# Attention with a relative position bias and a squared-ReLU layer: longer score matmuls, block diagonals, and x transposed by DMA

## Chip, core and metric

The kernel runs on one core of one Trainium2 chip. The time is the device time of one execution in microseconds (us). Before the change the median of three runs was 442.41 us (440.94 to 442.55). The engines are named as in the profile: PE (TensorE), PEld (its weight loads), ACT (ScalarE), DVE (VectorE), POOL (GpSimd), SP (SyncE). POOL and SP issue the DMAs.

## What is computed

Eight batches, eight heads, 576 positions, head size 64: attention with a bias that depends on the distance of query and key alone, then two dense layers on the 4608 tokens of 512 values, with a squared ReLU between them.

```python
scores = scale * np.matmul(q, k.transpose(0, 1, 3, 2))          # 8 x 8 x 576 x 576
scores = scores + bias.transpose(2, 0, 1)[None, :, :, :]        # bias_table[bucket(|i - j|)]
attn = np.exp(scores - max); attn = attn / attn.sum(-1)
x = np.matmul(attn, v)                                          # -> (4608, 512)
h = np.maximum(x @ w_in, 0.0)                                   # w_in 512 x 2048
return h * h @ w_out                                            # w_out 2048 x 512
```

Beyond a distance of 128 all pairs share one bucket, so the kernel multiplies the exponentials by a table only in a band around the diagonal, and leaves the common factor to the normalization. Inputs are float32, cast to fp16 by the load DMAs.

## The kernel before

**Work in pairs of heads.** A pair p is a batch b and two heads (`pair`, 32 of them). The q and k of a batch are staged by load DMAs from POOL (`stg`, two buffers). For each pair PE transposes five blocks of q and five of k against an identity (L504) into a PSUM bank `f`; ACT or DVE copies them out to `qt` and `kt` (L483, L485), with one head on partitions 0 to 63 and the other on 64 to 127. Scores come transposed, keys on partitions: for each of four key blocks and each half of the queries (288) two matmuls, one per head, each on its 64 rows of PE (L528), into one of two score buffers `st` of two banks each. The last 64 keys make a set of their own of four matmuls (L535). ACT takes the exponential of each set, 576 columns at a time, nine per pair (L554), into `pt` and `pm`. DVE multiplies the bands by the table (L574). PE then forms PV for five blocks of queries, in a first part of three and a second of two, into the single bank `pv` (L612, L619); a column of ones in v gives the sum of each row. DVE takes the reciprocal (L636) and writes normalized x (L641).

**The dense layers.** After the four pairs of a batch, `x_turn` transposes x in 20 blocks on PE (L663) and ACT or DVE copies it to `xt`, a ring of 2560 tokens. A group g is 512 tokens, nine in all: f1 is 16 times four matmuls of 512 columns (L758), ACT takes the ReLU (L778), DVE squares it into `g` (L786); f2 is 16 quarters of four matmuls (L707); ACT or DVE copies `y` out (L727, L733) and SP stores it (L741). Transposes, f1 and f2 share three banks `f`.

**The order.** Nothing is issued as it is written. Each step is an operation in a plan (`Plan`) with the engines that may do it, an estimated cost, its dependencies, its buffers and a due time; `schedule` repeatedly takes the operation that can start first, the due time deciding ties, and the program is emitted in the planned order. Each engine works through its own instructions in that order. A pair's due time grows by `FAST` for the first pairs and by `PERIOD` after that, and `after` forbids work too far ahead of it. On PE an operation has a mode: "r" and "q" are the score matmuls on half the rows, "f" is full-array work; the plan adds `SWITCH` where the mode changes.

**The start.** On SP the small bias table is loaded, one matmul spreads it over distances, DVE casts it (L289), SP writes it to DRAM (`t_bias`) and reads it back skewed (`tr_sb`, four DMAs, all at L243), and DVE copies it into the tables (L314, L323). POOL issues the loads: `load_pair` for batch 0, `load_qk`, `load_v`, and the weights. Loads wait for DVE's memsets, the weight loads for nothing.

Of the kernel before, what the change touches and what calls it, by code (L numbers as in the profile page):

```python
# [27 lines left out]
XR = 2560  # L28
# [43 lines left out]
LAT = {"PE": 200.0, "ACT": 90.0, "DVE": 90.0, "POOL": 120.0, "DMA": 0.0, "SP": 0.0}  # L72
SWITCH = 60.0


class Plan:
# [11 lines left out]
    def schedule(self):  # L88
        engines = ("PE", "ACT", "DVE", "POOL", "SP", "DMA")
# [57 lines left out]
    @staticmethod  # L147
    def _buf_time(op):
        t = 0.0
        for b in op.bufs:  # L150
            if b.slot is None:
                if not b.ring.free:
                    return float("inf")
                t = max(t, min(b.ring.free)[0])
        return t


def mm(n):
    return n / 2.4 + 2.5
# [11 lines left out]
def kernel(  # L171
# [37 lines left out]
    tr_sb = sb("tr_sb", [128, H, 384])  # L209
    tv_sb = sb("tv_sb", [H, 512])  # L210
    oh_sb = sb("oh_sb", [32, 512])
    NSTG, NQK, NPT, NV, NX, NGB, NRT, NY = 2, 5, 2, 3, 2, 2, 4, 3
    stg = [[sb(f"{n}s{i}", [128, 5, 512]) for n in "qk"] for i in range(NSTG)]
    qts = [sb(f"qt{i}", [128, S]) for i in range(NQK)]
    kts = [sb(f"kt{i}", [128, S]) for i in range(NQK)]
# [5 lines left out]
    xs = [sb(f"x{i}", [128, 5, 512]) for i in range(NX)]  # L221
    xt_sb = sb("xt", [128, 4, XR])
    gs = [sb(f"g{i}", [128, 16, GT]) for i in range(NGB)]
    rts = [sb(f"rt{i}", [128, GT]) for i in range(NRT)]
# [14 lines left out]
    def loader(eng_name, eng, out_, in_, packets, deps=(), bufs=(), due=0.0):  # L239
# [8 lines left out]
        return P.add({"DMA": packets * 27.0 / 16}, None, [issue], bufs, due), issue  # L248
# [4 lines left out]
    def load(eng_name, eng, out_, in_, packets, deps=(), bufs=(), due=0.0):  # L253
# [12 lines left out]
    l_bt = load("SP", nc.sync, const(bt_sb), const(bias_table), 32, due=0)  # L266
    l_far = load(
        "SP", nc.sync, const(far_sb), const(bias_table[NBK - 1 : NBK, :].to_broadcast([NBK, H])), 32, due=1
    )
    l_oh = load("SP", nc.sync, const(oh_sb), const(oh_d.ap()), 32, due=2)  # L270
    l_id = load("SP", nc.sync, const(id_sb), const(id_d.ap()), 128, due=3)
# [21 lines left out]
    o = load("SP", nc.sync, lambda: tdram.ap(), const(tv_sb), 64, [o])  # L293
    o = P.add({"SP": 2000.0}, None, [o])
# [6 lines left out]
            256,  # L301
# [31 lines left out]
    first = []  # L333
    for i in range(NSTG):
        for w in range(2):
            first.append(
                P.add({"DVE": 320.0}, lambda i=i, w=w: io(nc.vector.memset(stg[i][w][64:128, 4, :].bitcast(FP32), 0.0)), due=10 + i)
            )
    for i in range(NPT):
        first.append(P.add({"DVE": 90.0}, lambda i=i: io(nc.vector.memset(pts[i][:, PW:], 1.0)), due=20))  # L340
        first.append(P.add({"DVE": 90.0}, lambda i=i: io(nc.vector.memset(p4s[i][:, S:], 1.0)), due=20))
# [30 lines left out]
    def load_pair(b, w, hp):  # L372
        src = (q, k)[w]
        t = lambda: stg[b_stg[b].slot][w]
        ls = []
        for h in (2 * hp, 2 * hp + 1):
            ls.append(
                load(
                    "POOL", nc.gpsimd,
                    lambda h=h: t()[:, 0:4, ts(h, D)],  # L380
                    const(src[b, h, 0:512, :].rearrange("(t p) d -> p t d", p=128)),
                    512, first[0:4], [b_stg[b]], pdue(),
                )
            )
        ls.append(
            load(
                "POOL", nc.gpsimd,
                lambda: t()[0:64, 4, ds(128 * hp, 128)].rearrange("p (h d) -> p h d", d=D),
                const(src[b, 2 * hp : 2 * hp + 2, 512:576, :].transpose([1, 0, 2])),
                128, first[0:4], [b_stg[b]], pdue(),  # L390
            )
        )
        l_qk[b, w, hp] = ls
# [451 lines left out]
```

## Time and profile before

| | |
|---|---|
| median of 3 runs | 442.41 us (440.94 to 442.55) |
| the profiled execution | 443.17 us |
| its span, first to last instruction | 441.4 us |
| busy PE / ACT / DVE / POOL | 417.2 / 288.0 / 210.2 / 119.5 us |
| chain that ended last, by engine | PE 91%, DMA 3%, ACT 3%, DVE 2%, issue 1% |
| granted TensorE clock, mean | 0.996 |
| DMA | 29.24 MB in 122170 packets |

The profile is of one execution. "Busy" adds the durations of an engine's instructions; matmuls are pipelined, so a busy PE says only that one was under way. The chain is followed back from the last instruction, at each step to what released it. In a group's row, the text before the bar is line, engine, operation, output<-inputs, shapes and count; behind it stand the busy time and mean duration (ns), then the engine's idle time just before these instructions and who ended it. In the rows of stretches each engine has its busy time and its instruction count.

### The profile page before, as it was taken

Reading aid. Unit: us, or ns where it says so; the run is one execution under the profiler, and the core shown is the slowest. Engines: PE = TensorE matmul, PEld = TensorE weight load, DVE = VectorE, ACT = ScalarE, POOL = GpSimd, SP = SyncE. Lnnn points to the kernel's source line nnn. Section 1 sums busy time; section 2 is a strip of 40 time slices with the busy share of each in tenths; the row PEclk is TensorE's granted clock in tenths of the full one; section 3 lists DMA queues with packets and bytes.
Section 4 is the critical chain, followed back from the end, with each engine's and each line's share of the span. In section 5 each row is a group of like instructions: output and inputs, shape, how many; then the busy total and the mean of one; then the engine's idle time right before and its main releaser. Section 6 shows DMA issues by size and latency. Waiting matters only on the chain.

```text
span 441.4 us, 9092 instructions
## 1 busy us (share of the span) xinstructions
PE 417.2 (95%) x3713; PEld 209.7 (48%) x3713; DVE 210.2 (48%) x513; ACT 288.0 (65%) x495; POOL 119.5 (27%) x154
## 2 busy tenths in 40 slices
PE   1687999999999999999999999999999999999996
PEld 0265545554455445544454445544454454544442
DVE  3545556445555655455455446465544553352210
ACT  1657787667866876777767666685777766464421
POOL 7998569422162205230254007000000000000000
PEclk9998999999999999999999999999999999999999
DMA  9999999918091808980099009400010001000111
GB/s 131 159 87 165 190 166 122 137 29 76 2 133 28 74 1 74 108 55 24 26 133 79 1 25 113 68 1 25 25 50 1 25 24 49 25 25 25 48 49 72
DMA packets 122170, 29.24 MB, mean 66 GB/s; under 512 B 113896, under 2 KB 117008, under 8 KB 122128
## 3 DMA queue, kind: packets, MB, share of 16 engines
q0 software_dynamic: 115552, 18.36, 56.5%
q1 hardware_dynamic: 6576, 10.30, 6.7%
q8 instruction: 29, 0.48, 0.5%
q14 instruction: 13, 0.11, 0.1%
HBM read 37.55 MB, written 9.45 MB: 106 GB/s over the span
## 4 chain that ended last, share of the span: by engine, by line
PE 91%; DMA 3%; ACT 3%; DVE 2%; issue 1%; SPq 0%; ACTq 0%; DVEq 0%
PE f L707 30%; PE f L758 29%; PE st L528 11%; PE pv L619 9%; PE f L504 4%; PE pv L612 3%; PE st L535 3%; PE f L663 2%; ACT pt L554 2%; DMA tr_sb<-t_bias 1%; DMA t_bias<-tv_sb 1%; DMA oh_sb<-c_oh 1%; SPq L243 0%; DVE pt L574 0%; ACT y L727 0%
## 5 line engine op out<-in xcount | busy, mean ns | idle before, releaser
L554 ACT ACTIVATE pt<-st 128x576 f16<-128x576 f32 x256 | 157.3, 649 | 42.1 <-PE st L528 40.1
L707 PE MATMUL f<-w_out_sb,g 128*128 128x512 f16 x576 | 144.9, 380 | 0.4 <-ACT qt L483 0.3
L758 PE MATMUL f<-xt,w_in_sb 128*128 128x512 f16 x576 | 141.0, 380 | 0.9 <-DVE xt L485 0.4
L778 ACT ACTIVATE rt<-f 128x512 f16<-128x512 f32 x144 | 86.1, 598 | 57.1 <-PE f L758 53.2
L786 DVE TENSOR_TENSOR g<-rt 128x512 f16<-128x512 f16 x144 | 61.1, 425 | 100.6 <-ACT rt L778 100.4
L758 PEld LDWEIGHTS <-w_in_sb 128*128 128x128 f16 x576 | 51.0, 97 | 61.3 <-issue 3.8
L574 DVE TENSOR_TENSOR pt<-pt,tb_sb 128x512 f16<-128x512 f16 (+2 forms) x96 | 59.7, 623 | 40.7 <-ACT pt L554 37.7
L707 PEld LDWEIGHTS <-g 128*128 128x128 f16 x576 | 48.7, 98 | 60.8 <-issue 13.2
L528 PE MATMUL st<-qt,kt 64*128 64x288 f16 x512 | 66.2, 298 | 4.8 <-ACT pt L554 3.7
L243 POOL DMA_DIRECT2D qs<-in_q_dram x47 | 38.1, 834 | 101.4 <-PE f L504 98.1
L619 PE MATMUL pv<-va,pt 128*128 128x65 f16 x1280 | 57.2, 196 | 0.2 <-DVE pt L574 0.2
L619 PEld LDWEIGHTS <-pt 128*128 128x128 f16 x1280 | 52.6, 100 | 5.1 <-issue 0.7
L528 PEld LDWEIGHTS <-kt 64*128 64x128 f16 x512 | 20.2, 94 | 57.8 <-issue 52.9
L243 POOL DMA_DIRECT2D va<-in_v_dram x32 | 28.4, 916 | 43.0 <-PE pv L619 26.9
L243 POOL DMA_DIRECT2D ks<-in_k_dram x47 | 38.2, 858 | 6.3 <-DMA w_out_sb<-in_moe_w_out_dram 3.5
L612 PE MATMUL pv<-vm,pm 128*128 128x130 f16 x160 | 36.1, 225 | 0.2 <-DVE x L641 0.2
L641 DVE TENSOR_TENSOR x<-pv,r 128x384 f16<-128x384 f32 x64 | 31.4, 491 | 2.2
L554 ACT ACTIVATE pm<-st 128x576 f16<-128x576 f32 x32 | 20.8, 651 | 13.0 <-PE st L535 13.0
L636 DVE RECIPROCAL r<-pv 128x6 f32<-128x6 f32 x64 | 11.9, 187 | 26.0 <-PE pv L619 25.7
L727 ACT ACTIVATE y<-f 128x512 f32<-128x512 f32 x20 | 12.0, 598 | 18.6 <-PE f L707 18.2
L504 PE MATMUL f<-id_sb,qs 128*128 128x128 f16 x160 | 15.5, 234 | 4.3 <-DMA qs<-in_q_dram 4.3
L612 PEld LDWEIGHTS <-pm 128*128 128x128 f16 x160 | 15.9, 99 | 6.5 <-issue 1.4
(37 smaller groups left out, 175.7 us busy)
## 6 DMA issues: line engine op xcount, KB each, us to landing
out_dram<-y SPq DMA_DIRECT2D x36, 256.0 KB, 2.0
va<-in_v_dram POOLq DMA_DIRECT2D x32, 128.0 KB, 5.2
qs<-in_q_dram POOLq DMA_DIRECT2D x28, 128.0 KB, 4.6
ks<-in_k_dram POOLq DMA_DIRECT2D x28, 128.0 KB, 5.1
w_in_sb<-in_moe_w_in_dram POOLq DMA_DIRECT2D x4, 512.0 KB, 7.4
w_out_sb<-in_moe_w_out_dram POOLq DMA_DIRECT2D x4, 512.0 KB, 9.5
qs<-in_q_dram POOLq DMA_DIRECT2D x15, 64.0 KB, 4.8
ks<-in_k_dram POOLq DMA_DIRECT2D x15, 64.0 KB, 4.7
```

Of the source, the lines that this page charges most:

```text
L243: lambda: io(eng.dma_start(out=out_(), in_=in_())),
L504: io(nc.tensor.transpose(ps[:, ts(t, 128)], stg[b_stg[b].slot][w][:, t, ts(hp, 128)], id_sb))
L528: nc.tensor.matmul(ps[:, e, 0:HQ], kt[rows, ts(jt, 128)], qt[rows, ts(hh, HQ)], start=True, stop=True,)
L554: nc.scalar.activation(out=dst, in_=sets_ps[st.slot][:, :, 0:HQ], func=EXPF, scale=SCALE)
L574: io(nc.vector.tensor_tensor(out=a, in0=a, in1=t, op=MULT))
L612: nc.tensor.matmul(ps[:, i, :, :], pm[:, c : c + 128], vm[:, hp, :, 0:65], start=True, stop=False)
L619: nc.tensor.matmul(ps[:, i, e, :], pt[:, (2 * jt + e) * S + c : (2 * jt + e) * S + c + 128], va[:, jt, 2 * hp + e, 0:65], start=False, sto ...
L641: nc.vector.tensor_tensor(out=xs[xb.slot][:, qt0 : qt0 + nq, ts(hp, 128)].rearrange("p t (e d) -> p t e d", e=2), in0=ps[:, :, :, 0:64], i ...
L707: nc.tensor.matmul(g_ps[bank.slot], gs[gb.slot][:, nt, ts(m, 128)], w_out_sb[:, nt, :], start=(nt == 0), stop=(nt == 15),)
L758: nc.tensor.matmul(g_ps[bank.slot], w_in_sb[:, kk, ts(nt, 128)], xt_sb[:, kk, c : c + GT], start=(kk == 0), stop=(kk == 3),)
L778: nc.scalar.activation(out=rts[rb.slot], in_=g_ps[bank.slot], func=RELUF)
L786: nc.vector.tensor_tensor(out=gs[gb1.slot][:, nt, :], in0=rts[rb.slot], in1=rts[rb.slot], op=MULT)
```

## The change

**Scores.** The nine sets of a pair become six. A key block's set now has all of the first 512 queries: two matmuls of 512 columns, one per head on its 64 rows (L604 in the new file). Outside batch 0 the blocks are run two at a time, so that one visit fills both score buffers (`run([0, 1])`, `run([2, 3])`). The last 64 queries go against all four key blocks by four full-array matmuls of 128 columns (L628) with `qz`, in which the 64 last queries of each head stand on a block diagonal; the last 64 keys likewise by two matmuls of 288 columns with `kz` (L653). The off-diagonal blocks of `qz` and `kz` are zeroed once (four buffers each); per pair four copies of 64x64 fill the diagonals (L586), each on DVE or POOL as the plan finds. Exponentials are of 1024 columns (four per pair, L615), 512 (L638) and 576 (L663).

**x.** With `DT_X`, x is laid out per pair and each part of PV is followed by one DMA transpose from SBUF to SBUF, issued by SP (L779): 32 of three blocks and 32 of two. `x_turn` isn't called. `DT_QK = 8` leaves q and k on PE in all eight batches. `xt` is a ring of 2304 tokens; f1 of the one group that crosses its end (group 4) is cut into two times 256 columns.

**Loads.** In batches 0 and 1 q and k are loaded six positions to a partition (96 partitions, 1536 bytes of the source in a row), transposed by 12 matmuls of 96 columns on half the output partitions (L559), and put in order by the evacuating copy. In batches 2 to 7 a batch's q is ten DMAs (one per head, and two for the last 64 positions) in place of five, k the same. The first q and k no longer wait for memsets. POOL's order of loads is new, as the diff shows. The first reading of the table lies in the buffer of `g`, which group 1 overwrites after the table is copied.

**The plan.** New due times, `SWITCH` 105, latencies for DMAs and a new resource "XB" for the transposes; f2 and f1 wait for their own quarter of the weights and squares instead of all.

The diff, cut:

```diff
-XR = 2560
+XR = 4 * S
+DT_QK = 8
+PERIOD, LEAD, FAST, FASTN = 9700.0, 8100.0, 4800.0, 5
+AHEAD, G0, GP = 12500.0, 22300.0, 37900.0
+DT_X = True
...
-LAT = {"PE": 200.0, "ACT": 90.0, "DVE": 90.0, "POOL": 120.0, "DMA": 0.0, "SP": 0.0}
-SWITCH = 60.0
+LAT = {"PE": 200.0, "ACT": 90.0, "DVE": 90.0, "POOL": 120.0, "DMA": 1800.0, "SP": 0.0, "XB": 2000.0}
+SWITCH = 105.0
...
     for hp in range(4):
         for w in range(2):
-            load_pair(0, w, hp)
+            load_six(0, w, 2 * hp, 2)
         if hp == 1:
-            load_v(0)
+            load_v_tail(0, range(4))
+            for h in range(4):
+                load_v_head(0, h)
+    for h in range(4, 8):
+        load_v_head(0, h)
+    for u in range(4):
+        load_w_in(u)
     for w in range(2):
-        load_qk(1, w)
-    for kk in range(4):
-        load_w_in(kk)
+        load_six(1, w, 0, 4)
     load_v(1)
+    for w in range(2):
+        load_six(1, w, 4, 4)
     for u in range(4):
         load_w_out(u)
...
-    PERIOD, LEAD, FAST = 10300.0, 12000.0, 5900.0
...
+        spread = []
+        for w, src, dst in ((0, qts, qzs), (1, kts, kzs)):
+            for e in range(2):
+                rw = ds(64 * e, 64)
+
+                def sp(o, src=src, dst=dst, rw=rw):
+                    eng = nc.vector if o.eng == "DVE" else nc.gpsimd
+                    io(eng.tensor_copy(out=dst[qb.slot][rw, rw], in_=src[qb.slot][rw, 512:576]))
+
+                spread.append(one_of({"DVE": 130.0, "POOL": 300.0}, sp, [evac[w]] + z_fix, [qb], T - 1000))
...
+        def run(jts):
+            sets = [Buf(r_set) for _ in jts]
+
+            def score():
+                kt, qt = kts[qb.slot], qts[qb.slot]
+                for jt, st in zip(jts, sets):
+                    for e in range(2):
+                        rw = ds(64 * e, 64)
+                        io(
+                            nc.tensor.matmul(
+                                sets_ps[st.slot][:, e, :], kt[rw, ts(jt, 128)], qt[rw, 0:512],
+                                start=True, stop=True,
+                            )
+                        )
...
+        def last_queries():
+            st = Buf(r_set)
+
+            def score():
+                for jt in range(4):
+                    io(
+                        nc.tensor.matmul(
+                            sets_ps[st.slot][:, 0, ts(jt, 128)], kts[qb.slot][:, ts(jt, 128)], qzs[qb.slot],
+                            start=True, stop=True,
+                        )
+                    )
...
+        if b < 1:
+            run([0])
+            run([1])
+            last_keys()
+            run([2])
+            run([3])
+        else:
+            run([0, 1])
+            last_keys()
+            run([2, 3])
+        last_queries()
...
+            if DT_X:
+                c = (b % 4) * S + 128 * qt0
+                t = P.add(
+                    {"SP": 1000.0},
+                    lambda qt0=qt0, nq=nq, c=c: io(
+                        nc.sync.dma_start_transpose(
+                            out=xt_sb[:, hp, c : c + 128 * nq].rearrange("p (t d) -> p t d", d=128), in_=xs[xb.slot][:, hp, qt0 : qt0 + nq, :].rearrange("p t d -> p (t d)")
+                        )
+                    ),
+                    [o, x_last.get((hp, 1 - part))] + xt_free(b * S + 128 * (qt0 + nq)), [xb], T - 2000,
+                )
+                t = x_last[hp, part] = P.add({"XB": 160.0 * nq}, None, [t], [xb], T - 2000)
...
-        x_turn(b, norms)
+        if not DT_X:
+            x_turn(b, norms)
```

Where instructions come to stand, as the two programs are emitted. First PE in the middle of the program, before: a score visit between two f2 quarters (`g` and `w_out_sb`); `st` is a score buffer, `kt` the turned keys.

```order
L707 MATMUL f_114<-w_out_sb,g_100 128x512
L528 LDWEIGHTS kt_85
L528 MATMUL st_111<-qt_80,kt_85 128x288
L528 LDWEIGHTS kt_85
L528 MATMUL st_111<-qt_80,kt_85 128x288
L707 LDWEIGHTS g_100
```

After, in the same part of the work:

```order
L741 MATMUL pv_117<-va_96,pt_91 128x65
L604 LDWEIGHTS kt_82
L604 MATMUL st_115<-qt_78,kt_82 128x512
L604 LDWEIGHTS kt_82
L604 MATMUL st_115<-qt_78,kt_82 128x512
L604 LDWEIGHTS kt_82
L604 MATMUL st_116<-qt_78,kt_82 128x512
L604 LDWEIGHTS kt_82
L604 MATMUL st_116<-qt_78,kt_82 128x512
L844 LDWEIGHTS g_105
```

A visit holds four matmuls of 512 columns in place of two of 288, and follows PV or f2 as before.

Second, PE where f1 of group 3 begins, before; what an instruction waits for stands in brackets:

```order
L707 LDWEIGHTS g_99
L707 MATMUL f_115<-w_out_sb,g_99 128x512
L758 LDWEIGHTS w_in_sb
L758 MATMUL f_114<-xt,w_in_sb 128x512 [waits DVE_49]
L758 LDWEIGHTS w_in_sb
L758 MATMUL f_114<-xt,w_in_sb 128x512
```

After:

```order
L844 MATMUL f_118<-w_out_sb,g_104 128x512
L897 LDWEIGHTS w_in_sb [waits DMAHW1_49]
L897 MATMUL f_119<-xt,w_in_sb 128x512 [waits DVE_49]
L897 LDWEIGHTS w_in_sb
L897 MATMUL f_119<-xt,w_in_sb 128x512 [waits DMAHW3_49]
L897 LDWEIGHTS w_in_sb [waits DMAHW5_49]
L897 MATMUL f_119<-xt,w_in_sb 128x512 [waits DMAHW4_49]
L897 LDWEIGHTS w_in_sb [waits DMAHW7_49]
L897 MATMUL f_119<-xt,w_in_sb 128x512 [waits DMAHW1_49]
```

The waits on the copies of `xt` (DVE) are replaced by waits on DMA completions (DMAHW); the one on DVE that is left is for the bank.

Third, SP ahead of and among the output stores, before:

```order
L243 DMA t_bias<-tv_sb 8x512 [waits DVE_49]
L243 DMA tr_sb<-t_bias 128x2x384 [waits DMAHW4_49]
L243 DMA tr_sb<-t_bias 128x2x384 x2
L243 DMA tr_sb<-t_bias 128x2x384 [waits DMAHW0_49]
L741 DMA out_dram<-y_105 128x512 [waits DMAHW1_49,Activation_49]
L741 DMA out_dram<-y_106 128x512 [waits DMAHW2_49,DVE_49]
L741 DMA out_dram<-y_107 128x512 [waits DMAHW3_49,DVE_49]
```

After, with the transposes of batch 4:

```order
L779 DMA_TRANSPOSE xt<-x_101 128x3x128 [waits DMAHW4_49,DVE_49,PE_49]
L779 DMA_TRANSPOSE xt<-x_101 128x2x128 [waits DMAHW5_49,DVE_49,PE_49]
L878 DMA out_dram<-y_112 128x512 [waits DMAHW6_49,Activation_49]
L779 DMA_TRANSPOSE xt<-x_101 128x3x128 [waits DMAHW7_49,DVE_49]
L779 DMA_TRANSPOSE xt<-x_101 128x2x128 [waits DMAHW0_49,DVE_49,PE_49]
L779 DMA_TRANSPOSE xt<-x_101 128x3x128 [waits DMAHW1_49,DVE_49]
L878 DMA out_dram<-y_110 128x512 [waits DMAHW2_49,DVE_49]
```

The 64 transposes now stand among the 36 stores in one queue; a transpose waits for DVE's norm, for PE's last use of that part of the ring, and for the DMA eight places ahead, and a store that waits for `y` holds the transposes behind it.

On POOL, 45 of the 128 copies into `qz` and `kz` stand between the loads; the other 83 are on DVE. In batches 2 and later the copies stand right behind loads in five places, in four of them behind 20 or more.

364 lines of the change are left out of this document (209 added, 155 removed).

## Prediction

> **What bounds the kernel now.** I read the page's engine totals first, then its chain of work that ended last, then busy time by stage. The PE row and the chain by engine:
>
> ```profile
> PE 417.2 (95%) x3713; PEld 209.7 (48%) x3713; DVE 210.2 (48%) x513; ACT 288.0 (65%) x495; POOL 119.5 (27%) x154
> PE 91%; DMA 3%; ACT 3%; DVE 2%; issue 1%; SPq 0%; ACTq 0%; DVEq 0%
> ```
>
> PE carries 91% of a 441.4 us chain, about 402 us. Busy time in two stretches (length, then PE, PEld, DVE, ACT, POOL, granted clock, DMA share, GB/s) shows where the rest lies:
>
> ```profile
> 0.00:50.20 50.20, 31.34 (x357) 19.97 (x357) 25.15 (x77) 28.10 (x48) 42.01 (x60) 0.97 1.47 140
> 50.20:420.00 369.80, 368.29 (x3276) 181.95 (x3277) 183.78 (x434) 255.64 (x441) 77.45 (x95) 1.00 0.55 56
> ```
>
> From 50.2 us on PE is full (368.3 of 369.8 us), so the time there is the sum of PE's instructions, with ACT at 69% and DVE at 50%. The chain near 240 us (start, length, what; xN is matmuls) prices each kind:
>
> ```profile
> 234.40 0.23 PE st L528 x2
> 234.63 0.97 PE f L707 x4
> 235.60 0.22 PE f L663 x4
> 235.82 2.59 PE f L758 x12
> 238.41 0.35 PE st L528 x4
> 238.77 1.83 PE f L758 x8
> ...
> 241.80 0.29 PE f L504 x5
> ...
> 244.25 0.06 PE pv L612
> 244.31 0.24 PE pv L619 x8
> 244.55 0.86 PE f L758 x4
> 245.41 0.36 PE st L535 x4
> ```
>
> Twelve 512-column matmuls behind another full-array matmul take 2.59 us, 0.216 each. Four take 0.86 us behind PV, but 0.97 us behind scores: entering full-array work from scores costs 0.107 us more. Two 288-column score matmuls, on the two row halves, take 0.23 us, four take 0.35 us: a second pair adds 0.12 us (one 288-column stream, so the halves run together), and entering the scores costs the other 0.11 us. A change of kind, either way, is 0.107 us. A transpose is 0.056 us (0.22 over four, 0.29 over five), a 65-column PV matmul 0.03, a 130-column one 0.06.
>
> Now the instruction order, which has no times. Before has 383 such changes. Its columns at these prices sum to 364.2 us and 383 x 0.107 = 41.0, together 405.2 us, within 1% of the chain's 402. The same sum up to the first f1 matmul is 19.8 us; that matmul starts at 50.24 us, so 30.4 us are lost ahead of it. What is left of 441.4 is about 4 us at the end and 2 us between.
>
> **The change, part by part.** The profiled execution took 443.17 us, 1.77 more than its span; the median of the runs is 442.41, 0.76 less. I sum against 443.17 and take 0.76 off at the end.
>
> *Fewer changes of kind.* A pair now has two visits to row-tiled scores, mostly four 512-column matmuls at a time; the remaining queries and keys are full-array matmuls on block diagonals and need no change. The order has 144 changes (14 of them around the 96-column transposes of batches 0 and 1, priced alike). 239 x 0.107 = **-25.6 us**.
>
> *Score columns.* Tiled pairs: 256 x 0.1225 = 31.4 us become 128 x 0.216 = 27.6: -3.7. The last keys stay at 0.245 us per pair of heads (two 288-column streams). The last queries are new: 128 x 0.056 = +7.2. **+3.5 us**.
>
> *Transposes.* The 160 of x leave PE: 160 x 0.056 = **-9.0 us**. Those of q and k become 240 at 0.056 and 192 column-tiled ones of 96 columns, 28 ns each if their halves run together: 18.8 against 17.9, with the split f1 group **+1.1 us**.
>
> PE in all: -25.6 + 3.5 - 9.0 + 1.1 = **-30.0 us**, 375 us of work. It counts fully, since PE is full.
>
> *Other engines.* Mean durations of groups (busy us, mean ns):
>
> ```profile
> L554 ACT ACTIVATE pt<-st 128x576 f16<-128x576 f32 x256 | 157.3, 649 | 42.1 <-PE st L528 40.1
> L778 ACT ACTIVATE rt<-f 128x512 f16<-128x512 f32 x144 | 86.1, 598 | 57.1 <-PE f L758 53.2
> L641 DVE TENSOR_TENSOR x<-pv,r 128x384 f16<-128x384 f32 x32 | 17.8, 557 | 1.1
> L636 DVE RECIPROCAL r<-pv 128x6 f32<-128x6 f32 x32 | 6.2, 194 | 16.7 <-PE pv L619 16.6
> L354 DVE MEMSET vm<- 64x8 f16 x6 | 0.4, 65 | 0.3
> L323 DVE COPY tm_sb<-tr_sb 64x192 f16<-64x192 f16 x8 | 2.3, 288 | 0.1
> ```
>
> 64 more columns cost 51 ns, so a 1024-column exponential is about 1.01 us and a pair's six take 4 x 1.01 + 0.60 + 0.65 = 5.28 us against 9 x 0.649 = 5.84. ACT and DVE also lose the 40 evacuations of x. Neither is on the path after 50 us; this counts only at the start. The 128 new 64x64 copies lie between 65 and 288 ns each; 83 stand on DVE, 45 on POOL.
>
> *The start.* Chain pieces and two timeline rows:
>
> ```profile
> 6.80 4.76 DMA t_bias<-tv_sb
> 12.53 5.50 DMA tr_sb<-t_bias
> 25.79 0.22 PE pv L612
> 50.24 2.76 PE f L758 x12
> ```
>
> ```profile
> 1.24 1.25 POOL L243 DMA_DIRECT2D w_in_sb<-in_moe_w_in_dram  x2 [0.79 <-POOLq L829]
> 10.40 0.69 PE L504 MATMUL f<-id_sb,qs 128*128 128x128 f16 x5 [4.34 <-DMA qs<-in_q_dram]
> ```
>
> Before, two 512 KB weight loads stand ahead of the first q, and PE begins at 10.4 us. Now q and k stand first: I take 6.5 us. The table's road is the same two DMAs in series, so the first PV needs about 19 us instead of 25.8, and pair 1 is through at 24.5. Two pt buffers let pair 2's exponentials start only then: 2 x 5.28 = 10.6 brings 35, band and PV of the last pair 3.5, x to f1 4.1: 42.6 us. PE's own work ahead of it is 17.2 us, so 25.4 are lost against 30.4: **-5 us**, from -9 (PE begins at 5, lighter queues) to +2 (the table still decides, and x comes late).
>
> *The wait for x.* Only this kernel's other DMAs from SP bound it (duration of an issue, then of landing; both answers are for the output stores), with the identity's landing under the first loads as the far end:
>
> ```profile
> L741 SPq DMA_DIRECT2D out_dram<-y x36: 332/332/356, 79.9 to 438.3; - x36
> DMA to landing us min/median/max: 2.0/2.0/4.8
> ```
>
> ```profile
> id_sb<-c_id SPq DMA_DIRECT2D x1, 32.0 KB, 7.6
> q0 software_dynamic: 115552, 18.36, 56.5%
> ```
>
> From the end of PV: reciprocal 0.19, norm 0.56, issue 0.33 (one plain issue) to 1.0 (three, one a block), landing 2.0 to 4.8: 3.1 to 6.6 us. In the order, the work that PE still has between the last PV that a group needs and the group's first f1 is 6.9, 5.1, 6.2, 6.2, 5.1, 5.1, 4.9 and 16.4 us for groups 1 to 8 (before group 3: two score runs with their entry and exit 1.3, four quarters of f2 3.5, ten transposes 0.6, a PV part 0.6, the last keys 0.25). Group 0 has none; its wait is in the start. A light queue hides it all; a loaded one leaves 1 to 2 us at up to seven groups. The load queue holds 56.5% of the DMA time, so I take half of the groups at 1 us: **+3 us** (0 to +14). The stores on SP are no hindrance: 36 x 0.33 and 64 issues of at most 1 us are 76 us of 410.
>
> The page "VectorE: DVE Perf Modes" of the Trainium skill (section "The three transpose paths") speaks against this edit: 1309 ns for a 128x128 block through the DMA crossbar, 390 ns on TensorE. The second is not what this stream pays (0.056 us). By the first, an estimate is 3.9 us for three blocks, inside my landing range, and the term would be about the same +3.
>
> *Copies behind loads on POOL.* The q and k of a batch are now 20 loads instead of 10, and some copies that scores need stand right behind them, in a queue whose head waits for PE. From the waits, and the landing of such loads:
>
> ```profile
> POOL qs L243 <- PE f L504: 98.1, 4, 28.7
> va<-in_v_dram POOLq DMA_DIRECT2D x32, 128.0 KB, 5.2
> ```
>
> Each load waits for the one eight places ahead. 20 loads are 4608 packets each for q and k; at 34.5 ns (56.5% of 16 x 441.4 us over 115552 packets) on 16 engines they need 19.9 us, so the end of a burst can be some us later than 20 issues of 0.8. The order has five such places, four of them behind 20 loads or more. Above: 5 x 3; below: 0, if the copies are early. **+4 us**.
>
> *Longer runs need both score buffers at once*, so PE can wait for two exponentials (2 us) where it waited for one. f1 and f2 quarters stand between; the 3.7 us that L528 waited on ACT in all before is the nearest row: **+1** (0 to +6).
>
> ```profile
> L528 PE MATMUL st<-qt,kt 64*128 64x288 f16 x512 | 66.2, 298 | 4.8 <-ACT pt L554 3.7 <-ACT pm L554 0.4
> ```
>
> The end (last output evacuated and stored) is unchanged: 0.
>
> Sum: 443.17 - 30.0 - 5 + 3 + 4 + 1 = 416.2; less 0.76 is 415.4, rounded **415 us**.
>
> The page "TensorE: Matmul & The Clock Gate" of the Trainium skill (Part 1) says that an idle window of about 3.4 us halves PE's clock until it has been busy as long. By that rule the 4.1 us wait ahead of the first f1 would add an estimated 1.7 us. The trace agrees in so far as the clock fell to 0.84 at the start, where PE was busy for 8.44 of 11 us:
>
> ```profile
> 33.00:44.00 11.00, 8.44 (x110) 5.83 (x107) 6.29 (x16) 8.23 (x16) 9.43 (x13) 0.84 1.62 165
> ```
>
> **The rivals.**
> *Late transposes (slower).* Place: the first f1 of each group. If a transpose lands not after 3 us but after T, each of seven groups waits T + 1.25 (reciprocal, norm, issue) less 5.5 us (the mean work in between), and group 0 waits T - 3 more. The other terms save 30 us; slower by 0.5% needs 7 x (T - 4.25) + (T - 3) = 32, that is T = 8.1 us. The identity's 7.6 us comes near it; the stores' maximum of 4.8 us speaks against. At T = 10 it is 460 us.
> *Long row-tiled pairs do not overlap.* Then 128 x 0.216 = 27.6 us come back: 443 us. The 0.12 us of a 288-column pair speaks against.
> *POOL and ACT are late at every batch.* 5 us at each of five burst ends and 6 us for the buffers: 415 + 21 + 5 = 441 at the worst, some 433 in the middle. POOL's 28.7 us wait shows how long its queue can stand.
> *The start doesn't shorten:* 420 us, inside the range.
>
> **How the numbers follow.** The forecast's own range: 443.2 - 30 - 9 = 404, less 0.8 is 403, if nothing new waits; 443.2 - 30 + 2 + 14 = 429 if x is late in all groups. Chances: forecast 0.75, POOL and ACT late 0.12, pairs not overlapped 0.04, late transposes slower than before 0.07, better than 403 0.02. The range 402 to 431 holds the forecast and the nearer part of the third rival. Faster by over 0.5% (2.2 us, about what a measurement of this kernel can tell from no change): 0.75 + 0.12 + 0.02 = 0.89; the pairs' rival is the 0.04 within; slower 0.07.
>
> **What would show it.** Right: PE busy near 390 us or less, the first f1 at 40 to 45 us, four score matmuls of 512 columns at 0.43 us plus one entry in the chain, f1 waiting on the DMA of xt for under 14 us in all, PE full between. Wrong: the DMA of xt ahead of f1 with over 20 us in the waits (T too small), the last keys and queries waiting on POOL for over 10 us, or a four-matmul visit near 0.9 us.

## The result, and the profile after

The changed kernel takes 418.75 us (median, 418.23 to 419.54), the kernel before on the same chip 441.77 us. The ratio is 0.948, with a 95% interval from 0.945 to 0.951. The forecast was 415.0 us, from 402 to 431. The profiled execution took 418.23 us, its span is 416.5 us, 24.9 less than before.

First the engine totals and the chain of the changed kernel, to be laid beside those of before:

```profile
PE 386.6 (93%) x3537; PEld 210.6 (51%) x3537; DVE 213.1 (51%) x576; ACT 271.9 (65%) x387; POOL 157.8 (38%) x241
PE 80%; DMA 9%; POOL 7%; issue 2%; ACT 1%; POOLq 0%; ACTq 0%
```

PE is busy for 30.6 us less. But where DMA, ACT and DVE had 8% of the chain, DMA and POOL now have 16%. These pieces lie ahead of 75.3 us, where the chain runs through POOL's loads and their landings, then through the copies behind them (the two longest landings, and POOL's longest row of issues):

```profile
20.92 17.22 DMA va<-in_v_dram
40.81 13.97 DMA w_out_sb<-in_moe_w_out_dram
57.87 6.58 POOL ks L250 x9
```

Busy time by stage shows the same stretch (length, then PE, PEld, DVE, ACT, POOL, granted clock, DMA share, GB/s), in the changed kernel:

```profile
37.00:82.00 45.00, 31.49 (x310) 16.14 (x307) 20.07 (x52) 25.48 (x38) 34.30 (x51) 0.85 1.62 139
82.00:412.50 330.50, 329.94 (x2900) 178.67 (x2899) 167.17 (x432) 222.11 (x319) 100.00 (x155) 1.00 0.56 66
```

and in the kernel before, with the same borders:

```profile
37.00:82.00 45.00, 42.23 (x430) 23.07 (x428) 25.33 (x60) 34.47 (x61) 34.14 (x43) 0.96 1.84 161
82.00:437.80 355.80, 354.70 (x3096) 175.12 (x3094) 167.87 (x396) 234.64 (x405) 52.66 (x64) 1.00 0.41 48
```

From 82 us on PE is full in both, and all of the gain lies there: 330.5 us instead of 355.8. From 37 to 82 us PE was busy for 42.2 us and is now for 31.5, at a lower clock. PE's waits of 0.2 us and over in that stage, from PE's timeline of the changed kernel (start, length, what, and in brackets the idle time before it and who ended it):

```profile
40.79 0.61 PE L897 MATMUL f<-xt,w_in_sb 128*128 128x512 f16 x1 [3.20 <-DMA xt<-x]
45.70 6.12 PE L897 MATMUL f<-xt,w_in_sb 128*128 128x512 f16 x21 [4.31 <-DMA xt<-x]
64.78 0.88 PE L604 MATMUL st<-qt,kt 64*128 64x512 f16 x4 [0.78 <-ACT pm L663]
67.20 0.39 PE L604 MATMUL st<-qt,kt 64*128 64x512 f16 x2 [0.33 <-ACT pt L615]
69.73 0.22 PE L734 MATMUL pv<-vm,pm 128*128 128x130 f16 x1 [0.61 <-DVE x L763]
75.33 0.42 PE L653 MATMUL st<-qt,kz 128*128 128x288 f16 x2 [3.33 <-POOL kz L586]
```

The first f1 starts at 37.0 us (50.24 before). Two pieces of x come late, 7.5 us in all, and the last keys of a pair wait 3.3 us for a POOL copy. The waits for x are not on the chain above: by it, an earlier x alone would only have PE wait longer for the copy, unless POOL's loads end earlier too. PE's largest waits over the whole run show that both happen in the start and never again (us in total, times, longest):

```profile
PE f L897 <- DMA xt<-x: 7.5, 2, 4.3
PE f L289 <- DMA oh_sb<-c_oh: 4.3, 1, 4.3
PE st L653 <- POOL kz L586: 3.3, 1, 3.3
PE st L604 <- ACT pm L663: 2.0, 4, 0.8
PE pv L741 <- DVE pt L696: 1.9, 3, 0.7
PE st L604 <- ACT pt L615: 1.8, 5, 0.5
```

A simple account follows from the first f1 of group 1, which is the point where PE becomes full. It starts at 100.08 us, before at 100.03 us. In the instruction order PE's work ahead of that point is 61.9 us at the prediction's prices, before 68.75; behind it 313.2 us, before 336.4. So:

| | before | after | difference |
|---|---|---|---|
| PE's work ahead of group 1's first f1 | 68.75 | 61.9 | -6.85 |
| lost ahead of group 0's first f1 (50.24 - 19.8; 37.0 - 17.2) | 30.4 | 19.8 | -10.6 |
| lost between these two | 0.9 | 18.4 | +17.5 |
| from group 1's first f1 to the end of the span | 341.4 | 316.4 | -25.0 |
| span | 441.4 | 416.5 | -24.9 |

The first three rows cancel. Of the 18.4 us, PE's waits of 0.2 us and over make 13.4 (7.5 for x, 3.3 for POOL's copy); an estimated 3.3 us more are a low granted clock behind these two waits, as worked out further down. In the stretch where PE is full, the prices give -23.2 us and the trace -25.0.

Three pieces of the chain of the changed kernel, from that stretch, show the score runs themselves:

```profile
100.94 0.54 PE st L604 x4
103.31 0.24 PE st L653 x2
105.28 0.22 PE st L628 x4
```

Four 512-column score matmuls take 0.54 us: 0.43 for two streams of 512 columns and 0.107 for entering, so the row halves run together. The block diagonals have no entry to pay: 0.24 us for two matmuls of 288 columns, 0.22 for four of 128.

### The profile page after: what moved, and what is told of

Same layout as the page of the kernel before. It is cut to its first block, busy times and chain, and to the rows that moved or that the text cites. A ratio compares the mean times of both kernels' runs of the same rounds, so it can differ in the third digit from the quotient of the medians.

```text
span 416.5 us, 8915 instructions
## 1 busy us (share of the span) xinstructions
PE 386.6 (93%) x3537; PEld 210.6 (51%) x3537; DVE 213.1 (51%) x576; ACT 271.9 (65%) x387; POOL 157.8 (38%) x241
## 4 chain that ended last, share of the span: by engine, by line
PE 80%; DMA 9%; POOL 7%; issue 2%; ACT 1%; POOLq 0%; ACTq 0%
PE f L844 30%; PE f L897 27%; PE pv L741 8%; PE st L604 7%; DMA va<-in_v_dram 4%; PE f L566 4%; DMA w_out_sb<-in_moe_w_out_dram 3%; POOL ks L250 2%; POOL va L250 2%; PE pv L734 2%; DMA ks<-in_k_dram 2%; PE st L653 2%; PE st L628 1%; POOL qs L250 1%; POOL vm L250 1%
## 5 line engine op out<-in xcount | busy, mean ns | idle before, releaser
L615 ACT ACTIVATE pt<-st 128x1024 f16<-128x1024 f32 x128 | 125.3, 1022 | 37.7 <-PE st L604 37.6
L897 PE MATMUL f<-xt,w_in_sb 128*128 128x512 f16 (+1 forms) x640 | 139.1, 361 | 7.7 <-DMA xt<-x 7.5
L897 PEld LDWEIGHTS <-w_in_sb 128*128 128x128 f16 x640 | 60.6, 98 | 67.5 <-issue 8.7
L250 POOL DMA_DIRECT2D qs<-in_q_dram x66 | 47.1, 750 | 47.8 <-PE f L566 36.6
L250 POOL DMA_DIRECT2D ks<-in_k_dram x66 | 47.4, 821 | 0.8 <-DMA ks<-in_k_dram 0.8
L604 PE MATMUL st<-qt,kt 64*128 64x512 f16 x256 | 42.9, 402 | 4.7 <-ACT pm L663 2.0
L864 ACT ACTIVATE y<-f 128x512 f32<-128x512 f32 x30 | 17.9, 598 | 25.6 <-PE f L844 25.3
L586 POOL COPY qz<-qt 64x64 f16<-64x64 f16 x23 | 10.2, 444 | 63.4 <-DVE qt L524 58.6
L663 ACT ACTIVATE pm<-st 128x576 f16<-128x576 f32 x32 | 20.8, 651 | 8.0 <-PE st L653 6.7
L586 POOL COPY kz<-kt 64x64 f16<-64x64 f16 x22 | 7.0, 319 | 39.6 <-DVE kt L524 27.5
L604 PEld LDWEIGHTS <-kt 64*128 64x128 f16 x256 | 8.7, 95 | 23.9 <-issue 20.6
```

The lines of the kernel that those rows point to most:

```text
L250: lambda: io(eng.dma_start(out=out_(), in_=in_())),
L604: nc.tensor.matmul(sets_ps[st.slot][:, e, :], kt[rw, ts(jt, 128)], qt[rw, 0:512], start=True, stop=True,)
L615: nc.scalar.activation(out=p5(pts[pb.slot])[:, jt, :, 0:512], in_=sets_ps[st.slot], func=EXPF, scale=SCALE)
L663: nc.scalar.activation(out=p4s[pb.slot][:, 0:S].rearrange("p (h s) -> p h s", h=2), in_=sets_ps[st.slot][:, :, 0:HQ], func=EXPF, scale=SCALE,)
L897: nc.tensor.matmul(g_ps[bank.slot][:, a:z], w_in_sb[:, kk, ts(nt, 128)], xt_sb[:, kk, c : c + z - a], start=(kk == 0), stop=(kk == 3),)
```

## Experiments

Theory after the result: the gain is the scores' (fewer changes of kind on a full PE), and what was gained on the way to the first f1 is given back right behind it, because x lands late beside the loads and POOL's copies stand behind loads. Rivals: the gain comes from taking x off PE; the losses in the start are ACT's and no queue's; the transposes are slow wherever they stand. "The changed kernel" is the kernel of the diff above; its rows keep its line numbers, and the versions that hold back loads have three lines more ahead of these. PE's work is counted in each order at the prediction's prices. Every ratio is to the kernel before on the same chip, with its 95% interval.

**The changed kernel once more.** 

> The changed kernel as it is, as the yardstick for the three kernels beside it on the same chip: 418.7 us by every theory (418.2 to 419.5 before). The first f1 stalls twice on the DMA of xt (about 3.2 and 4.3 us), the pair at 71 us on the copy into kz (3.3 us).

Measured: 418.48 us, ratio 0.946 (0.944 to 0.948). Here too x was waited for twice (7.4 us) and POOL's copy once (2.5 us).

**The scores as before, the rest as changed.** The scoring loop of the kernel before (nine sets a pair, eight of two matmuls of 288 columns and the last keys' of four, no `qz` and `kz`) in place of the new one:

```diff
-        run([0, 1])
-        last_keys()
-        run([2, 3])
-        last_queries()
+        for jt in (4, 0, 1, 2, 3):
+            for half in range(2) if jt < 4 else (0,):
...
```

> The scores as before the change (288 columns, nine sets a pair, last keys on 64 rows, no block diagonals and no copies into them), everything else of the change kept, the DMA transposes of x too. The order has 369 changes of kind and 395.8 us of PE work against 144 and 375.1. Theory (the scores are most of the gain): +20.7, less the 3 us that PE waited for the copies: 436 to 440 us. Rival (the gain came from x and from the loads at the start): under 430 us.

Measured: 442.49 us, ratio 1.001 (1.000 to 1.003), over both. The new scores are worth 24 us, all of the gain. The 369 changes that I expected leave out those between the last keys' matmuls and the other score matmuls, which are among the prediction's 383. They cost an entry too: in the chain of this kernel the two matmuls of L592 at 133.59 us, right behind the last keys' four, take 0.23 us, which is one pair of 288 columns, 0.12, and 0.11 for entering. With the 23 of these there are 392 changes and 398.3 us of work, so 23.2 of the 24 us are PE's work in the order. The losses differ by only 1 us: the span exceeds PE's work by 42.4 us here and by 41.4 in the changed kernel. The wait for POOL's copy is gone, but PE waits 6.0 us at L592 for exponentials, where the changed kernel waits 3.8 at L604. DMA transposes, loads and plan together bring nothing.

**x on TensorE.** The constant that decides it:

```diff
-DT_X = True
+DT_X = False
```

> The changed kernel with x turned on TensorE again (160 transposes on PE, 40 copies on ACT and DVE; no DMA transposes). The order has 144 changes of kind as before this edit, and 384.1 us of PE work against 375.1. Theory (PE is full after 82 us, so work there counts fully; ahead of that the DMA transposes cost about 7.5 us of waiting, of which a turn on PE gives back some 5): 418.5 + 9 - 5 = 422 to 424 us. Rival 1 (the wait for x would be filled by the loads of batch 1 anyway): 427 us. Rival 2 (turning x by DMA brought nothing): 419 us or less.

Measured: 423.49 us, ratio 0.960 (0.956 to 0.963), as the theory had it. The 9.0 us of transposes are back, and 4.3 us of losses go (span less PE's work: 421.2 - 384.1 = 37.1 us, against 41.4). So turning x by DMA is worth 5 us by the medians (5 to 6 by the ratios), about half of what it takes off PE. Put beside the run before it: new scores bring 24 us and DMA transposes 5, together 29, and the changed kernel gained 23. If the parts add up, the new loads and plan cost some 6 us, which no run here measured by itself.

**Runs of one key block in all batches.** This takes back the pairing alone, so that 53 changes of kind return:

```diff
-        if b < 1:
+        if b < 8:
             run([0])
             run([1])
```

> Score runs of one key block at a time in all batches, not two; the same matmuls otherwise. The order has 197 changes of kind against 144, so 380.8 us of PE work against 375.1 us. Theory (a change costs 0.107 us and PE is full): 424 us. Rival (what a longer run costs is the wait for both score buffers, so that single runs free PE): 418 us or less.

Measured: 419.97 us, ratio 0.951 (0.948 to 0.954): 1.5 us slower than the changed kernel, where the work is 5.7 more, between theory and rival. Behind group 1's first f1 (at 91.39 us here) the prices hold: 326.2 us to the end of the span against 322.3 of work, 3.9 more; in the changed kernel 3.2 more. Ahead of it only 32.9 us are lost (91.39 - 58.5) instead of 38.2. So 5.7 us more work, 0.7 more lost behind that point and 5.3 less ahead of it make the 1.1 us by which the two spans differ. PE's waits lack the one for POOL:

```profile
PE f L897 <- DMA xt<-x: 8.2, 3, 4.6
PE st L604 <- ACT pt L615: 3.6, 7, 1.4
```

So the price of a change stands where PE is full, and the rival's wait does not shrink: PE waits 4.0 us for exponentials at L604 (3.6 in the row above, and 0.4 for `pm`), in the changed kernel 3.8. Why less is lost in the start, and why the POOL copies came in time in this order, was not followed up.

**The copies on DVE.** The first of three attempts on the losses in the start; the order on PE stays:

```diff
-                spread.append(one_of({"DVE": 130.0, "POOL": 300.0}, sp, [evac[w]] + z_fix, [qb], T - 1000))
+                spread.append(one_of({"DVE": 130.0}, sp, [evac[w]] + z_fix, [qb], T - 1000))
```

> The copies into qz and kz all on DVE, 45 more of 0.18 us there. PE's order and its 144 changes of kind stay. Theory (copies stand behind loads in POOL's queue, and PE waits for that): the 3.3 us wait of the last keys near 71 us goes, PE's clock drops less, 415 us. Rival (PE would wait there for loads or for ACT anyway): 418 to 419. If DVE is the tighter queue after all: above 419.5.

Measured: 417.92 us, ratio 0.944 (0.942 to 0.947): no difference that can be told from the changed kernel. The theory missed. The wait for POOL is gone, and PE waits as long a microsecond earlier, as its timeline shows:

```profile
74.28 0.22 PE L734 MATMUL pv<-vm,pm 128*128 128x130 f16 x1 [3.14 <-DVE x L763]
```

DVE's timeline shows what stands ahead of the normalization that frees PV: five copies that take 2.5 us. At the 0.18 us of the median copy in the changed kernel they would have taken 0.9; here they take 0.4 to 0.75 us each, while POOL issues loads:

```profile
70.90 0.75 DVE L586 COPY qz<-qt 64x64 f16<-64x64 f16 x1
71.66 0.87 DVE L586 COPY kz<-kt 64x64 f16<-64x64 f16 x2
72.55 0.86 DVE L586 COPY qz<-qt 64x64 f16<-64x64 f16 x2
73.44 0.20 DVE L758 RECIPROCAL r<-pv 128x6 f32<-128x6 f32 x1
73.67 0.56 DVE L763 TENSOR_TENSOR x<-pv,r 128x384 f16<-128x384 f32 x1
```

and POOL's timeline the loads of that time:

```profile
70.57 3.70 POOL L250 DMA_DIRECT2D va<-in_v_dram  x4
```

**The later loads held back.** A small POOL copy that reads the last piece of batch 0's x stands ahead of the loads of batch 1's second half, of `w_out` and of all that follow, so that the first transposes have the DMA engines with less beside them:

```diff
+    held = [o for o in P.ops[held_from:] if "POOL" in o.engs]
...
+        if b == 0:
+            gate = P.add(
+                {"POOL": 200.0}, lambda: io(nc.gpsimd.tensor_copy(out=hold_sb, in_=xt_sb[:, 3, 448:512])),
+                [x_last[3, 1]], (), 0.0,
+            )
+            for o in held:
+                o.deps.append(gate)
```

> A copy on POOL that reads the last transposed block of batch 0 is put ahead of the second half of batch 1's q and k, of w_out and of all later loads, so that these wait until that transpose has landed. Theory (transposes of batch 0 land after 7 to 8 us because the DMA engines are full of loads): the last ones land in 4.5 us or less, f1's fourth matmul starts at 42.5 us or earlier in place of 45.7. POOL's queue is then some 4 us later, so that the gain is partly given back at the copies near 71 us: 416, and not under 414. Rival (the landing time is the transposes' own, or that of the loads issued earlier): landing stays at 7 us or more, and the time is 419 to 422.

Measured: 415.8 us (413.4 to 419.7), ratio 0.940 (0.936 to 0.944). The profiled execution took 414.1 us. The landing of the four transposes issued from 30 to 45 us, in the changed kernel and then with the loads held back (us, shortest, median, longest):

```profile
DMA to landing us min/median/max: 7.0/7.4/7.8
```

```profile
DMA to landing us min/median/max: 2.3/2.7/6.5
```

The median falls to a third, and PE's wait for x from 7.5 to 2.4 us. But this run alone does not test the theory on x, for x was issued later too. PE's timeline has a new wait for POOL's copies ahead of the first f1, which begins at 41.53 us instead of 36.99:

```profile
34.58 0.66 PE L656 MATMUL st<-qt,kz 128*128 128x288 f16 x2 [2.76 <-POOL kz L589]
44.72 4.69 PE L900 MATMUL f<-xt,w_in_sb 128*128 128x512 f16 x21 [2.38 <-DMA xt<-x]
```

The last two transposes were issued at 40.9 and 42.4 us (36.4 and 37.9 in the changed kernel), when all loads that were not held back had landed. f1's fourth matmul, which needs the last piece of x, begins at 44.72 us, in the changed kernel at 45.70; I had expected 42.5 or earlier.

**Both.** The two edits above together, loads held back and the copies on DVE:

> Both: copies on DVE, and the loads held until batch 0's last transpose has landed. Theory (two separate waits, each on the path): the gains add, 411 to 413 us. Rival (what comes next, the loads of batch 1 and w_out, ends at the same time in all of them): 415 to 419.

Measured: 412.73 us, ratio 0.934 (0.932 to 0.937), 5.8 us under the changed kernel with the same work on PE. This is the test of the theory on x, for here the last two transposes are issued when they were in the changed kernel, at 36.4 and 37.9 us. They land after 5.3 and 4.0 us instead of 7.5 and 7.8, and f1's second wait of 4.3 us is gone: the loads beside them did slow these two. The two ahead of them, issued when loads that were not held back were still landing, take 6.7 and 8.0 us. PE's waits are now 3.8 us for x, once, and 2.3 us of PV for DVE:

```profile
41.49 7.00 PE L900 MATMUL f<-xt,w_in_sb 128*128 128x512 f16 x22 [3.83 <-DMA xt<-x]
68.12 0.22 PE L737 MATMUL pv<-vm,pm 128*128 128x130 f16 x1 [2.33 <-DVE x L766]
```

**The copies planned at 400 ns.** The kernel of the last run with a DVE copy put into the plan at what it took there:

```diff
-                spread.append(one_of({"DVE": 130.0}, sp, [evac[w]] + z_fix, [qb], T - 1000))
+                spread.append(one_of({"DVE": 400.0}, sp, [evac[w]] + z_fix, [qb], T - 1000))
```

> The fastest kernel so far (412.7) with the DVE copies of the block diagonals put into the plan at 400 ns instead of 130, about what they took there while POOL issued loads; 143 changes of kind, 375.0 us of PE work. If PV's wait of 2.3 us near 68 us is due to where the plan puts the copies on DVE, it goes: 410 to 411. If the plan's order does not decide it (DVE is slow whatever the plan says), 412 to 413.5.

Measured: 412.8 us, ratio 0.936 (0.932 to 0.939), no gain. The wait of 2.33 us became one of 0.95, so the plan's order did decide that wait; but the time stayed, so the expectation that hung on it fell. Longer waits for `kt` (2.9 us in three, before 0.7) and for DVE at L744 (2.5, before 1.6) came in its place:

```profile
PE st L607 <- ACT kt L525: 2.9, 3, 1.3
PE f L900 <- DMA xt<-x: 2.5, 2, 2.3
PE pv L744 <- DVE pt L699: 2.5, 3, 1.4
```

**The first batch's x on TensorE, the rest by DMA.** If the transposes cost time in the start alone, they should be left out there alone:

```diff
-            if DT_X:
+            if DT_X and b > 0:
...
-        if not DT_X:
+        if not DT_X or b == 0:
             x_turn(b, norms)
```

> The changed kernel with the x of the first batch alone turned on TensorE (20 transposes), all later batches by DMA; 376.2 us of PE work instead of 375.1. Theory, that the DMA turn costs time only where x lands behind the start's loads: the two waits of 7.5 us for x and some 2 us of the low clock behind them go, 1.1 us of PE work comes: 418.5 - 7.5 - 2 + 1.1 = 410, from 408 to 413, and no wait for x in any later group. Rival, that the loads on POOL set the pace of the start anyway: PE only reaches the last keys of batch 1 earlier, where its wait for POOL's copies grows from 3.3 to some 9 us: 416 to 419.

Measured: 413.85 us, ratio 0.938 (0.936 to 0.940), some 4 us under the changed kernel (whose ratios are 0.946 and 0.948), between the two, nearer to the theory. PE waits for x by DMA in no group, although 56 transposes are still issued. Its largest wait on POOL is the queue that the rival named, at half the size that the theory left it:

```profile
69.83 0.58 PE L628 MATMUL st<-qz,kt 128*128 128x128 f16 x4 [1.80 <-POOL qz L586]
```

By POOL's timeline the loads ahead of the copy end at 69.3 us instead of 74.0, so that the wait did not grow as the rival had it. Between 42 and 55 us POOL waits mostly for its own `w_out` loads to land, in both kernels, and not for PE. So the loads still set the pace of POOL's queue; they land earlier in this kernel, where no transposes of x stand beside them. That the transposes had slowed them was not tested by itself.

**The same with the copies on DVE.** 

> The kernel with the first batch's x on TensorE, and all copies of the block diagonals on DVE besides; the same PE order. If POOL's loads ahead of the copies are what is late next, the wait of the last keys goes and the time is 3 us under that kernel or more: 407 to 409 where that one is at 410 to 412, and 412 or less where that one stays at 416 or over. Rival, as when the copies alone were moved to DVE: they stand ahead of the norm there and PV waits for x instead, so the two kernels agree within 1 us.

Measured: 411.57 us, ratio 0.931 (0.928 to 0.934): 2.3 us less than with the copies on POOL, between the rival's 1 and the theory's 3, nearer to the theory. The wait for POOL is gone, and this time DVE has room: no wait of PE for DVE is over 1.0 us.

**The same with the loads held back too**, behind the first batch's x as TensorE turned it. 

> The fastest kernel so far (copies on DVE, the later loads held back until the first x is there; 412.7) with the first batch's x on TensorE. Theory, that the DMA turn's remaining cost there is its wait of 3.8 us and some low clock: 412.7 - 3.8 - 1 + 1.1 = 409, from 408 to 410.5. Rival, that the loads held back until then come too late for batch 1, so that what is gained is lost at the wait for DVE near 68 us: 412 to 413.

Measured: 411.46 us, ratio 0.933 (0.931 to 0.935), about a microsecond less by the medians than with x by DMA in all batches (the intervals of the ratios overlap), half a microsecond below the rival's range and one above the theory's. It cannot be told from the run before it: with the first x on TensorE, holding loads back brings nothing that shows. By their medians these two are the fastest kernels here; like the two at 412.7 and 412.8 us they beat both the kernel before and the changed one. The last one's PE waits, behind the 4.4 us for a load ahead of all work, are all small:

```profile
PE pv L744 <- DVE pt L699: 2.4, 4, 0.7
PE st L631 <- ACT pt L618: 2.3, 4, 1.0
PE st L656 <- ACT pt L618: 1.5, 2, 0.9
```

**Each transpose issued twice.** The second copy writes the same values behind the first's landing, so that x comes about twice as late:

```diff
-                    lambda qt0=qt0, nq=nq, c=c: io(
+                    lambda qt0=qt0, nq=nq, c=c: [io(
...
-                    ),
+                    ) for _ in range(2)],
```

> Every DMA transpose of x issued twice, one behind the other's landing, PE's order unchanged: the time T to x's landing doubles. By the sum of the late-transposes rival: T = 7 in the loaded stretches gives 2 us at each of six groups, 8 us at group 1, which needs both parts, and 12 to 18 us at group 0, where a landing takes 7.4 us now: 440 to 455 us. Rival (the work ahead of each f1 hides much more than I counted, the cost is in the start alone): 430 to 436 us. If x has slack everywhere: 419 us.

Measured: 504.66 us, ratio 1.141 (1.135 to 1.148), 50 us beyond what I expected. The largest wait of PE and of SP's queue:

```profile
PE f L897 <- DMA xt<-x: 80.0, 12, 15.2
```

```profile
SPq L779 <- DMA xt<-x: 134.2, 64, 7.0
```

PE's wait for x grows by 72.5 us of the 82 by which the span grows. PE is also busy for 12 us longer, at a mean clock of 0.911 instead of 0.980. My expectation had each x late by one more landing. But the second copy waits on SP's queue for the first to land, and everything behind it in that queue waits too: 64 waits, 134 us. The eight pieces of batch 0 thus went one after the other, and group 0 alone waited 40.6 us (6.2, 15.2, 11.0 and 8.2). The run shows how dear a late x is, not what one landing of twice the length would cost.

## Why the prediction was right, point by point

The forecast of 415 us was 3.75 us low, and its sum names the right term. Several of its parts were off, in opposite directions, so that the total came out so near is in part luck.

*Fewer changes of kind*, *score columns*, *transposes* (-30.0 us of PE's work): right. Where PE is full, 23.2 us by prices came out as 25.0 us. The 0.54 us of four score matmuls is 0.43 and one entry, as foreseen, so the rival that long pairs don't overlap is out. The old scores gave back all of the gain, and in the single runs the price of an entry held wherever PE was full.

*The start* (-5 us, to -9): the road was right up to the exponentials. ACT had those of batch 0's last pair done at 34.6 us, where the sum had 35. 10.6 us fewer were lost ahead of the first f1, which came at 37.0 us instead of 42.6. Most of the difference is the 4.1 us from x to f1: the first matmul of f1 needs x of one pair alone, so this wait came behind it, and the fourth matmul, which needs all four pairs, began at 45.70 us. So the point itself was badly chosen. The first f1 is not the end of the start: behind it lie the other pieces of x and batch 1, and 17.5 us were lost there which before were not. The prediction held PE to be full from the first f1 on, and looked for losses at each batch instead.

*The wait for x* (+3, half of the later groups at 1 us): the size of the term is off, and so is its place. It is 7.5 us, all of it in group 0, and nothing in the later groups. The prediction said "Group 0 has none; its wait is in the start", and had 4.1 us for it there. The landing was sized by the output stores, 2.0 to 4.8 us, all of them issued after 79 us, when the first burst of loads is over. In the start the transposes landed after 7.0 to 8.0 us, beside the loads; the longest row at hand, the identity's 7.6 us under the first loads, was the right one for that place, and was used only as the far end and for the rival. Later the landings are as the stores', in the changed kernel over all 64 and over those issued from 280 to 380 us:

```profile
L779 SPq DMA_TRANSPOSE xt<-x x64: 1167/1179/1745, 20.1 to 356.1; - x64
DMA to landing us min/median/max: 2.3/3.7/8.0
```

```profile
DMA to landing us min/median/max: 2.3/2.3/4.0
```

and the 4.9 to 16.4 us of work between PV and f1 hide them in all eight groups. The rule of 1309 ns a block, from the page "VectorE: DVE Perf Modes" of the Trainium skill (section "The three transpose paths"), gave an estimate of 3.9 us for three blocks. The trace does not bear out a price by the block: the pieces of three and of two blocks issued at 295.0 and 296.6 us both land after 2.3 us, and in the start 7 to 8 us are needed. That the median over all pieces is 3.7 us is chance.

The late x also lowers the clock, a cost for which the sum had no term. Stretches of the changed kernel around the second wait (columns as above):

```profile
41.40:45.70 4.30, 0.00 (x0) 0.10 (x1) 0.00 (x0) 0.00 (x0) 2.88 (x5) 0.50 1.26 197
45.70:48.70 3.00, 3.00 (x8) 1.08 (x8) 0.47 (x2) 1.19 (x2) 0.74 (x1) 0.51 1.24 206
48.70:51.80 3.10, 3.10 (x17) 1.25 (x17) 1.41 (x4) 1.79 (x3) 0.74 (x1) 1.00 1.24 207
```

For 3 us behind the wait the granted clock is 0.51; the 21 matmuls there took 6.12 us instead of 21 x 0.216 = 4.5, so 1.6 us more. The page "TensorE: Matmul & The Clock Gate" of the Trainium skill (Part 1) says that an idle window halves the clock until PE has been busy for as long, about 3.4 us. The trace agrees here, and the estimate of 1.7 us that the prediction worked out from it for one such wait, and kept out of its sum, is about what was paid.

*Copies behind loads on POOL* (+4): the size is near, 3.3 us, but by luck, for it was paid at none of the five places counted. Those are in batches 2 and later, whose q and k PE turns (L566) from 89.26 us on; the copy waited for at 75.33 us is of batch 1, behind loads for later batches. From 84 us on PE waits for no POOL copy. The granted clock is 0.64 and 0.58 in the two stretches of 2.2 us behind the wait, an estimated 1.7 us more (2.2 x 0.36 + 2.2 x 0.42). The runs with the copies on DVE showed that this wait is not alone: another, on DVE, came in its place, and the copies on DVE brought a gain only together with another measure.

*Both score buffers* (+1): PE's waits for the exponentials at L604 are 3.8 us in all (2.0 and 1.8), before 4.1. Nothing to be seen.

In sum: -30 - 5 + 8 = -27 was forecast for the span, -24.9 came. The start was 5.6 us better than forecast up to the first f1, the losses behind it were 9.5 us worse, and the full stretch was 1.8 better than its prices. The rival of late transposes was rightly kept at a small chance, but its deciding landing of 8.1 us was nearly met, for the one batch in which the loads are heavy.

## What to carry to other kernels

Where PE is full, count its instructions by kind and the changes between kinds in the order, price each from one stretch of the chain, and the difference holds within 2 us in 25. The start is over only where PE becomes full, not at the first instruction of the next stage, and a wait taken away there is replaced by what is late next: here the copy, then DVE. The copies on DVE alone brought nothing that can be told, the loads held back alone 2.7 us, both together 5.8. Size a transfer that is new by the landing of a transfer under the load of the place where it will stand, and where that load is heavy, leave the step on the engine: x on TensorE for the first batch alone, with the copies on DVE, gave some 6 to 7 us more (411.6 against 418.5).

## What the runs showed of the hardware

- A DMA transpose of two or three blocks takes SP 1.18 us to issue (median of 64), more than the 1.0 us at most that the prediction had, and lands after 2.3 us with light traffic and after 7.0 to 8.0 us with the start's loads beside it.
- DVE's 64x64 copies differ widely, in the changed kernel from 0.16 to 0.77 us:

```profile
L586 DVE COPY kz<-kt x42: 164/178/774, 7.2 to 338.3; 64x64 f16<-64x64 f16 x42
```

  The long ones of the run with all copies on DVE lie where POOL was issuing loads. That these issues are the cause was not tested by itself.
- The clock can be low without a long wait of PE. With the first x on TensorE and loads held back, PE had no wait over 1.0 us between 50 and 66 us, and yet:

```profile
57.00:60.00 3.00, 1.93 (x22) 1.04 (x21) 0.94 (x3) 3.00 (x6) 2.10 (x3) 0.96 1.93 126
60.00:63.00 3.00, 2.55 (x29) 1.58 (x26) 1.99 (x4) 3.00 (x5) 3.00 (x6) 0.50 1.16 74
63.00:66.00 3.00, 3.00 (x62) 2.79 (x60) 1.75 (x4) 1.70 (x3) 3.00 (x5) 0.50 1.38 88
```

PE was busy for 1.93 of 3 us ahead of it, and the granted clock was 0.50 for the next 6 us.
